# Sketches with the tokens as weights, a split decode and a new order in a sketched-attention and expert-attention kernel

## The chip, the cores and the metric

The kernel runs on one core of a Trainium2 chip. The metric is the device time of one execution in microseconds (us). The engines are PE (TensorE matmuls), PEld (its weight loads, which overlap PE), DVE (VectorE), ACT (ScalarE), POOL (GpSimd) and SP, which here issues most of the DMAs.

## What is computed

Two blocks in a row, for four batches. The first is linear attention on sketches: q and k (4 heads of 32) are projected by S1 and S2 onto 8 numbers each, and their 64 products are the features. The second takes the first one's output as x and computes causal attention for four experts, of which each token takes two.

```python
def phi(x):
    a = np.einsum('rd,bhsd->bhsr', S1, x)
    b = np.einsum('rd,bhsd->bhsr', S2, x)
    return np.einsum('bhsi,bhsj->bhsij', a, b).reshape(*x.shape[:-1], r * r)
q_p, k_p = (phi(q), phi(k))
kv = np.einsum('bhsf,bhsd->bhfd', k_p, v)
z = np.sum(k_p, axis=2)
num = np.einsum('bhsf,bhfd->bhsd', q_p, kv)
den = np.einsum('bhsf,bhf->bhs', q_p, z)[..., None] + 1e-06
x = num / den                       # (4, 4, 1088, 32) -> (4, 1088, 128)
logits = x @ w_gate                 # the two largest of four, softmax over them
for e in range(4):
    scores = scale * (x @ wq[e]) @ (x @ wk[e]).transpose(0, 2, 1)   # causal
    ye = softmax(scores) @ (x @ wv[e]) @ wo[e]
    out += weight_of_e_for_the_token * ye
```

All of it is float32, apart from S1 and S2, which arrive as float64.

## The kernel before

The program is a list of jobs (`job(name, engine, cost, function, reads, makes, holds)`), and `ORDER` is one written-out order of them, which gives every engine its own in-order queue. Words such as `77a` and `17b` are a job's number and which of its possible engines runs it. A buffer of a pool (`in`, `w`, `fp`, `AT`, the four PSUM pairs `ps`) is taken at a holder's first job and given back at its last. Costs and ranks in the jobs are those with which the order was made; at run time only the order counts.

The first batch (b = 0) is prepared alone, before anything else can run, and has its own code (`early`). In order:

- S1 and S2 arrive as pairs of 32-bit words; `decode` (DVE, L302 to L322) makes a high and a low float32 part and transposes them to `SK`, and `spread` copies them to all four row groups.
- k is loaded in two halves by rows (L422), q in twelve pieces (L459), v in four (L435). DVE turns k and q in blocks of 32 x 32 (L499, L511), so that the 32 numbers of a head lie on partitions.
- `sketch` (L538, L550) multiplies with 32 x 32 tiles, S as the weights and the tokens moving, high and low part added in PSUM. DVE turns the results back (L554, L563), and DVE and POOL multiply the features (L560, L568).
- `sums` (L626) adds features times v over tokens, by pairs of heads. It needs k's features and `vp`, which ACT and POOL spread from the loaded v (`spread v`). `keep sums` copies them to `kvz`.
- q's features are transposed on PE (`turn qf`, L669) and copied; `numer` (L689) multiplies them, 128 tokens as weights, by `kvz`; `divide` (L696 to L698), `turn x` (L704) and `keep x` make the turned x of a group of 6 or 5 times 64 tokens.
- The gate's logits (L902) need `wg`, which POOL copies from load w4. DVE compares and chooses (L906 to L948). The choices of group 0 are spread as masks by PE (`widen`); those of groups 1 and 2 go through DRAM (`store masks` L1008, `fetch masks` L1024).

After that the main stream runs per batch and group of tokens: `query` (L1089), `pick` on DVE by the masks (L1102), `score` (L1127), `take` on DVE (L1139, bias and maximum), `exp` on ACT, `weigh` on POOL, `turn A` on DVE (L1175), `sum` on PE (L1203), `out` (L1325). Batch b + 1 is prepared within it by other code (`add low`, `gram`, `fifth`, `numer` at L843). Forty `dummy` jobs (L255) are matmuls on zeros that the order may place on PE, or leave out (`b`).

## Time and profile before

| | us |
|---|---|
| median of 3 runs | 263.31 (262.7 to 264.98) |
| the profiled execution | 263.23 |
| its span | 261.1 |

| engine | busy us | share of the span |
|---|---|---|
| PE | 252.5 | 97% |
| DVE | 206.5 | 79% |
| POOL | 157.6 | 60% |
| ACT | 106.4 | 41% |

The busy times are those of the profiled execution; dummies count as busy. Times in timelines and in the chain count from the start of the span. "Idle before" is the time for which an engine did nothing ahead of an instruction, with what ended it.

### The profile page before, as it was taken

Reading aid. Unit: us, or ns where it says so; the run is one execution under the profiler, and the core shown is the slowest. Engines: PE = TensorE matmul, PEld = TensorE weight load, DVE = VectorE, ACT = ScalarE, POOL = GpSimd, SP = SyncE. Lnnn points to the kernel's source line nnn. Section 1 sums busy time; section 2 is a strip of 40 time slices with the busy share of each in tenths; the row PEclk is TensorE's granted clock in tenths of the full one; section 3 lists DMA queues with packets and bytes.
Section 4 is the critical chain, followed back from the end, with each engine's and each line's share of the span. In section 5 each row is a group of like instructions: output and inputs, shape, how many; then the busy total and the mean of one; then the engine's idle time right before and its main releaser. Section 6 shows DMA issues by size and latency. Waiting matters only on the chain.

```text
span 261.1 us, 9695 instructions
## 1 busy us (share of the span) xinstructions
PE 252.5 (97%) x4028; PEld 189.3 (72%) x4031; DVE 206.5 (79%) x529; ACT 106.4 (41%) x280; POOL 157.6 (60%) x258
## 2 busy tenths in 40 slices
PE   8899899999999999999999989999999999999994
PEld 2686564565598797485689956946796885789994
DVE  4858998999979988989987379999589759972342
ACT  3035653464701704563543145464513614541420
POOL 5850769689676773568963466666475354623470
PEclk9999999999999999999999999999999999999999
DMA  4683839896465329801802599232303059671003
GB/s 143 156 164 89 136 57 252 207 142 114 125 116 108 90 57 203 213 18 53 200 6 36 99 205 189 68 82 66 74 3 86 6 86 227 115 160 25 5 1 85
DMA packets 85467, 27.85 MB, mean 107 GB/s; under 512 B 56624, under 2 KB 84784, under 8 KB 85424
## 3 DMA queue, kind: packets, MB, share of 16 engines
q1 hardware_dynamic: 85120, 26.90, 49.8%
q8 instruction: 31, 0.51, 0.9%
q10 hardware_dynamic: 304, 0.35, 0.5%
q14 instruction: 12, 0.10, 0.1%
HBM read 22.62 MB, written 4.62 MB: 104 GB/s over the span
## 4 chain that ended last, share of the span: by engine, by line
PE 81%; DMA 6%; DVE 4%; SPq 4%; POOL 2%; issue 2%; ACT 0%; ACTq 0%; DVEq 0%; POOLq 0%
PE pair L1203 28%; PE pair L1127 23%; PE pair L1089 9%; PE pair L1325 7%; PE pair L1274 3%; DMA in<-in_q_dram 2%; DMA xd<-w 2%; DMA in<-in_k_dram 1%; PE pair L843 1%; DMA vp<-in_v_dram 1%; PE pair L550 1%; SPq L724 1%; DVE w L1139 1%; PE pair L1300 1%; PE pair L689 1%
## 5 line engine op out<-in xcount | busy, mean ns | idle before, releaser
L1170 POOL TENSOR_SCALAR w<-w,rs,sh 128x128 f32<-128x128 f32 (+15 forms) x68 | 56.1, 830 | 32.8 <-DVE rs L1166 31.4
L1155 ACT ACTIVATE w<-w,mx 128x448 f32<-128x448 f32 (+16 forms) x68 | 52.3, 770 | 56.9 <-DVE mx L1139 40.9
L1127 PE MATMUL pair<-xT,qs 128*128 128x448 f32 (+11 forms) x216 | 73.5, 478 | 0.9 <-DVE qs L1102 0.7
L1127 PEld LDWEIGHTS pair<-xT,qs 128*128 128x128 f32 x216 | 38.1, 190 | 26.1 <-issue 12.4
L1175 DVE STREAM_TRANSPOSE AT<-w 128x256 f32<-128x256 f32 (+14 forms) x68 | 50.8, 759 | 6.4 <-POOL w L1170 6.3
L1139 DVE CUSTOM_DVE_ANT_0 w<-pair,mask 128x768 f32<-128x768 f32 (+13 forms) x68 | 48.0, 723 | 4.5 <-PE pair L1127 3.5
L1203 PE MATMUL pair<-AT,xra 32*128 32x160 f32 (+5 forms) x1136 | 45.0, 302 | 0.0
L1203 PEld LDWEIGHTS pair<-AT,xra 32*128 32x128 f32 x1136 | 42.2, 185 | 3.7 <-DVE mx L1139 0.6
L1230 POOL TENSOR_TENSOR agg<-agg,mb 128x768 f32<-128x768 f32 (+1 forms) x22 | 33.9, 1559 | 13.4 <-ACT agg L197 9.9
L197 ACT COPY agg<-pair 128x384 f32<-128x384 f32 (+1 forms) x38 | 15.9, 469 | 51.6 <-PE pair L1203 41.1
L1089 PE MATMUL pair<-xT,Mq 128*128 128x384 f32 (+1 forms) x96 | 33.5, 474 | 0.1
L1203 PE MATMUL pair<-AT,xrb 32*128 32x160 f32 (+5 forms) x752 | 27.1, 286 | 0.0
L1102 DVE COPY_PREDICATED qs<-mb,pair 128x768 f32<-128x768 uint16 (+1 forms) x24 | 23.1, 961 | 4.6 <-ACT qs L197 2.6
L1203 PEld LDWEIGHTS pair<-AT,xrb 32*128 32x128 f32 x752 | 26.6, 185 | 0.0
L1089 PEld LDWEIGHTS pair<-xT,Mq 128*128 128x128 f32 x96 | 17.5, 190 | 11.1 <-issue 2.4
L568 POOL TENSOR_TENSOR fp<-w 128x576 f32<-128x576 f32 x20 | 23.8, 1204 | 1.9 <-DVE w L563 0.8
L1325 PEld LDWEIGHTS pair<-Mo,agg 128*128 128x128 f32 x168 | 20.1, 192 | 2.0 <-issue 1.0
L1325 PE MATMUL pair<-Mo,agg 128*128 128x128 f32 x168 | 20.7, 276 | 0.0
L1163 POOL TENSOR_SCALAR rs<-zs 128x1 f32<-128x1 f32 x33 | 8.1, 244 | 19.3 <-ACT w L1155 17.2
L1166 DVE RECIPROCAL rs<-rs 128x1 f32<-128x1 f32 x68 | 8.9, 141 | 9.0 <-ACT rs L1161 7.7
L1226 DVE COPY_PREDICATED agg<-mb,pair 128x384 f32<-128x384 uint16 (+1 forms) x24 | 12.5, 554 | 4.3 <-ACT agg L197 4.1
L197 ACT COPY qs<-pair 128x384 f32<-128x384 f32 (+1 forms) x22 | 9.3, 454 | 9.9 <-PE pair L1089 6.5
(180 smaller groups left out, 299.2 us busy)
## 6 DMA issues: line engine op xcount, KB each, us to landing
xra<-xd SPq DMA_DIRECT2D x16, 192.0 KB, 4.4
xrb<-xd SPq DMA_DIRECT2D x16, 192.0 KB, 4.8
xrc<-xd SPq DMA_DIRECT2D x16, 160.0 KB, 5.4
mb<-me SPq DMA_DIRECT2D x3, 576.0 KB, 5.4
mb<-me SPq DMA_DIRECT2D x6, 288.0 KB, 3.8
in<-in_k_dram SPq DMA_DIRECT2D x12, 136.0 KB, 3.5
in<-in_q_dram SPq DMA_DIRECT2D x3, 544.0 KB, 5.6
xd<-w SPq DMA_DIRECT2D x12, 136.0 KB, 3.6
```

Of the source, the lines that this page charges most:

```text
L197: (nc.scalar.copy if eng == "ACT" else VEC[eng].tensor_copy)(o, i)
L568: VEC[e].tensor_tensor(out=f, in0=a[:, :, None, R : 2 * R].to_broadcast([128, NJ, R, R]), in1=a[:, :, 0:R, None].to_broadcast([128, NJ, R, ...
L1089: nc.tensor.matmul(plan[ps[x]][:, y, 0:w], Mq[:, ((1, 2), (0, 3))[x][y]], plan[xT][:, 64 * t0 : 64 * t1], start=True, stop=True)
L1102: nc.vector.copy_predicated(chosen(), rows(c), rows(plan[ps[x]]))
L1127: nc.tensor.matmul(plan[p][:, y, 0 : c1 - c0], plan[qs][:, 128 * t : 128 * t + 128], plan[xT][:, c0:c1], start=True, stop=True)
L1139: nc.vector.tensor_tensor_reduce(out=o, in0=src, in1=msk, scale=-1.0, scalar=mx[:, b, i, x - 1 : x] if x else 3e38, op0=ALU.add, op1=ALU.m ...
L1155: nc.scalar.activation(out=a, in_=a, func=ACTF.Exp, bias=mx[:, b, i, last : last + 1], scale=-1.0, accum_out=zs[:, b, i : i + 1])
L1170: nc.gpsimd.tensor_scalar(out=a, in0=a, scalar1=rs[:, b, i : i + 1], scalar2=plan[("sh", b)][:, i : i + 1], op0=ALU.mult, op1=ALU.mult)
L1175: nc.vector.transpose(dst[:, 0 : keys // 32, t], plan[A][:, 0:keys].rearrange("p (j s) -> p j s", s=32))
L1203: nc.tensor.matmul(plan[Vk[g // 2]][:, g % 2, lo : 32 * nt], plan[(f"xr{j // 12}", b)][rows, j % 12], a[rows, j, lo:], start=(j == 0), sto ...
L1230: nc.gpsimd.tensor_tensor(out=a, in0=a, in1=plan[mb][:, 2 * x : 2 * x + 2, 0:w], op=ALU.mult)
L1325: nc.tensor.matmul(plan[p][0:m, 0, 128 * x : 128 * x + 128], plan[agg][:, e, 128 * x : 128 * x + m], Mo[:, e], start=(e == 0), stop=(e == ...
```

## The change

For the first batch alone:

- The sketches are turned round: 32 turned tokens are the weights (all four heads on 128 rows), and a block-diagonal copy `SB` of S (4 heads x 16 columns, once for the high and once for the low part) moves. The results come out with the tokens on partitions, so the transposes back are gone; `keep ab` copies them, and DVE's features read one operand from PSUM. k is done in two parts (blocks 0 to 4 and 5 to 8), q in three.
- The decode is in two jobs, high part first; `SB` is zeroed and filled by eight small copies. q's first sketch is in two jobs, high part first.
- k is loaded in four parts of 160, 160, 128 and 96 columns twice per row, into a buffer of `AT`, and turned in two parts that match the sketches. Its padding is zeroed before the turn.
- The sums go by token blocks (first five, then four) and no longer by pairs of heads.
- Each numerator's weights are 64 columns twice in place of 128 once.
- `ORDER` is new throughout. In the first 45 us: six dummy jobs lead (eleven matmuls) and none follows until two behind the last output (before: ten lead, ten lie between). v's loads have fifteen SP issues ahead (before fourteen). All of turn qf but one piece stands before the sums; numer 0.0 and 0.1 follow each other; `add low 1.1` is POOL's; load w4 stands behind the four loads of k1; POOL's one-hot and mask stand behind its part of the spread of v; `turn choice 0.1` stands before turn q1.0; the first fetch of x stands right behind the masks' fetches. Behind 57 us PE's groups follow each other as before, with scores and outputs changing places among themselves.

The core of the diff (the order itself and the job declarations are left out):

```diff
-            eng.dma_start(out=dst[:, c0:c1], in_=src[b].rearrange("h (t c) d -> (h t) (c d)", c=C)[:, c0:c1])
+            n, m = x // 2, x % 2
+            w = D * (5 - n - n * m)
+            src = k[b].rearrange("h (t c) d -> (h t) (c d)", c=C).rearrange("p (a y) -> p a y", a=2)
+            dst = plan[kin][:, 0 : 128 * NJ].rearrange("p (a g y) -> p a g y", a=2, g=2)[:, :, m]
+            eng.dma_start(out=dst[:, :, 160 * n : 160 * n + w], in_=src[:, :, 288 * m + 160 * n : 288 * m + 160 * n + w])
...
-                            nc.tensor.matmul(plan[ts[h // 2]][32 * g : 32 * g + 32, h % 2, 0:96], SK[rows, s],
-                                             src[rows, 384 * n + 96 * g : 384 * n + 96 * g + 96], start=(s == 0), stop=(s == 1))
...
+        def sketch_rows(nm, at, step, j0, j1, t, ss):
+            for s in ss:
+                for j in range(j0, j1):
+                    for g in range(4):
+                        c = at + 32 * (step * g + j)
+                        nc.tensor.matmul(plan[t][32 * g : 32 * g + 32, 0, 64 * (j - j0) : 64 * (j - j0) + 64], plan[turned_of(b, nm)][:, c : c + 32],
+                                         SB[:, s].rearrange("p h y -> p (h y)"), start=(s == 0 and j == j0), stop=(s == 1 and j == j1 - 1))
+
+        def keep_ab(e, nm, j0, j1, t):
+            copy(e, plan[ab[nm]][:, 64 * j0 : 64 * j1], plan[t][:, 0, 0 : 64 * (j1 - j0)])
+
+        def multiply(e, nm, j0, j1, at, t):
+            a = plan[ab[nm]][:, 64 * j0 : 64 * j1].rearrange("p (n y) -> p n y", y=16)
+            c = a if e == "POOL" else plan[t][:, 0, 64 * (j0 - at) : 64 * (j1 - at)].rearrange("p (n y) -> p n y", y=16)
...
-        def sums(m):
+        def sums(j0, j1):
...
-                nc.tensor.matmul(plan[t][:, z // 6, c : c + 2 * (D + 1)], f[:, y],
-                                 plan[kvz][:, y % 2].rearrange("p x d -> p (x d)"), start=True, stop=True)
+                for g in range(2):
+                    nc.tensor.matmul(plan[t][64 * g : 64 * g + 64, z // 6, c : c + 2 * (D + 1)], f[:, y, 64 * g : 64 * g + 64],
+                                     plan[kvz][:, y % 2].rearrange("p x d -> p (x d)"), start=True, stop=True)
```

## Rows read from the trace of the kernel before

**Rows 1.** The page, busy time, share and instructions of PE

```profile
PE 252.5 (97%) x4028; PEld 189.3 (72%) x4031; DVE 206.5 (79%) x529; ACT 106.4 (41%) x280; POOL 157.6 (60%) x258
```

**Rows 2.** The chain that ended last: start us, us, what

```profile
14.49 2.46 PE pair L626 x71
...
57.69 2.41 PE pair L1127 x6
```

**Rows 3.** Busy time by stretches: PE, PEld, DVE, ACT, POOL, PEclk, DMA share, GB/s

```profile
17.00:25.00 8.00, 8.00 (x99) 6.23 (x99) 5.69 (x21) 4.51 (x10) 1.10 (x3) 1.00 0.50 123
25.00:33.00 8.00, 7.09 (x81) 4.73 (x72) 7.75 (x26) 4.65 (x9) 5.11 (x12) 1.00 0.77 127
33.00:43.00 10.00, 9.94 (x183) 6.47 (x184) 8.90 (x40) 5.58 (x23) 7.72 (x15) 1.00 0.51 116
43.00:57.50 14.50, 13.86 (x216) 8.69 (x215) 13.51 (x25) 6.17 (x16) 11.99 (x22) 1.00 1.00 206
57.50:257.80 200.30, 198.99 (x3109) 153.99 (x3106) 159.35 (x387) 81.92 (x215) 119.96 (x176) 1.00 0.46 95
```

**Rows 4.** The same for the dummies (L255) alone: PE, then PEld

```profile
25.00:60.00 35.00, 2.35 (x7) 0.78 (x8) 1.00 0.78 153
```

**Rows 5.** Timeline of the start: start us, us, engine, instruction, [idle before]

```profile
4.25 0.23 DVE L322 STREAM_TRANSPOSE SK<-w 32x64 f32<-32x64 f32 x1
...
5.06 0.15 PEld L255 LDWEIGHTS <-idle 128*128 128x128 bf16 x1 [0.28 <-issue]
5.49 0.54 PEld L255 LDWEIGHTS <-idle 128*128 128x128 bf16 x3 [0.28 <-issue]
```

**Rows 6.** Timeline of v and the sums, and the landing of v's loads

```profile
7.54 1.86 SPq L435 DMA_DIRECT2D w<-in_v_dram  x4
DMA to landing us min/median/max: 2.7/3.4/4.1
...
13.17 1.07 ACT L197 COPY vp<-w 128x1024 f32<-128x1024 f32 x1 [8.15 <-DMA w<-in_v_dram]
...
14.49 2.35 PEld L626 LDWEIGHTS pair<-vp,fp 128*64 128x64 f32 x72 [0.42 <-ACT vp L197]
```

**Rows 7.** Timeline of PE: sketches of q, logits, Gram matmuls

```profile
12.44 0.88 PE L538 MATMUL pair<-w,SK 32*32 32x96 f32 x55 [0.71 <-issue]
...
22.70 0.53 PE L902 MATMUL pair<-xT,wg 128*32 128x192 f32 x8
...
31.87 0.35 PE L770 MATMUL pair<-w,bp 128*32 128x32 f32 x18 [0.48 <-DVE qs L1102]
```

**Rows 8.** DMA issues by tile: count, KB each, median us to landing

```profile
in<-in_k_dram SPq DMA_DIRECT2D x1, 272.0 KB, 3.9
...
wgr<-in_moe_w_gate_dram SPq DMA_DIRECT2D x1, 2.0 KB, 4.0
```

**Rows 9.** Timeline of PE's weight loads: one numerator of three

```profile
17.70 1.42 PEld L689 LDWEIGHTS pair<-kvz,fp 128*128 128x128 f32 x12
```

**Rows 10.** Timeline of DVE from the first division to the first pick by fetched masks

```profile
19.30 0.17 DVE L696 TENSOR_SCALAR den<-pair 128x12 f32<-128x12 f32 x1 [0.86 <-PE pair L689]
...
20.24 0.41 DVE L560 TENSOR_TENSOR fp<-w 128x256 f32<-128x256 f32 x1
...
23.38 0.38 DVE L906 STREAM_TRANSPOSE ch<-pair 128x192 f32<-128x192 f32 x1 [0.53 <-PE pair L902]
...
29.75 1.05 DVE L598 TENSOR_TENSOR w<-w 128x288 f32<-128x288 f32 x1
...
33.56 0.30 DVE L997 STREAM_TRANSPOSE cT<-c 64x128 bf16<-64x128 bf16 x1
33.80 0.24 DVE L1139 CUSTOM_DVE_ANT_0 w<-pair,mask 128x128 f32<-128x128 f32 x1
...
43.44 1.01 DVE L1102 COPY_PREDICATED qs<-mb,pair 128x768 f32<-128x768 uint16 x1 [1.04 <-DMA mb<-md]
```

**Rows 11.** Timeline of SP: the masks' two fetches

```profile
36.67 2.29 SPq L1024 DMA_DIRECT2D mb<-md  x2
```

More of the change, by code (lines that the diff above doesn't have):

```diff
@@ L527, in parts_ab, with sketch @@
             return plan[ab[nm]].rearrange("p (h j y) -> p h j y", h=H, j=NJ)
[L529 removed]
+        def sketch(nm, first_, ts):
             src = plan[turned_of(b, nm)]
[L532 to L540 removed]
+            both = nm == "k"
             for s in range(1 if both else 2):
@@ new lines, in sketches, with rows @@
+                    ("ah", nm, b, x) if nm == "k" else ("ab", nm, b, x), [ts[x], ab[nm]], rank=at + 0.5 + 0.1 * x)
+        def rows(nm, x, at, step, j0, j1, cuts_, need, r):
+            t, n = ("ps", "sk", nm, x), 64 * (j1 - j0)
+            base = j0 if nm == "k" else 0
+            cut = ((0,), (1,)) if nm == "q" and x == 0 else ((0, 1),)
+            for ss in cut:
+                last = ss[-1] == 1
+                job(f"sketch {nm}{b}.{x}" + ("" if last else " hi"), "PE", 0.13 * (j1 - j0) * len(ss), lambda e, ss=ss: sketch_rows(nm, at, step, base, base + j1 - j0, t, ss),
+                    [*need, *[("SB", s) for s in ss], *([("skh", nm, b, x)] if ss == (1,) else [])],
+                    ("sk" if last else "skh", nm, b, x), [turned_of(b, nm), t], mode="L", rank=r)
+            job(f"keep ab {nm}{b}.{x}", ("ACT", "DVE"), (a_us(n), d_us(n)), lambda e: keep_ab(e, nm, j0, j1, t),
+                [("sk", nm, b, x)], ("ab", nm, b, x), [t, ab[nm]], rank=r + 0.05)
+            for y, (c0, c1) in enumerate(cuts_):
+                w = 256 * (c1 - c0)
+                job(f"features {nm}{b}.{x}.{y}", ("DVE", "POOL"), (0.12 + w / 960, 0.12 + 0.00184 * w), lambda e, c0=c0, c1=c1: multiply(e, nm, c0, c1, j0, t),
+                    [("ab", nm, b, x)], ("fp", nm, b, x, y), [t, ab[nm], fps[nm]], rank=r + 0.2 + 0.1 * y)
@@ L618, in prepare @@
-        kvb = ("ps", "kv", b)
-        def sums(m):
-            t = plan[kvb][:, 0, 0 : 2 * (D + 1)].rearrange("p (m d) -> p m d", m=2)
-            kp = plan[fps["k"]].rearrange("p (j h f) -> p j h f", h=H, f=R * R)
-            for j in range(NJ):
-                for x in range(2):
-                    h = 2 * m + x
-                    nc.tensor.matmul(t[64 * x : 64 * x + 64, m], kp[:, j, h], plan[vp][:, j, h, :],
+        if early:
+            for x in range(2):
+                rows("k", x, 0, 9, kcuts[x][0][0], kcuts[x][1][1], kcuts[x], [("kT", b, x)], rank(0.05 + 0.01 * x))
+            for n in range(3):
+                rows("q", n, 384 * n, 3, 3 * n, 3 * n + 3, ((3 * n, 3 * n + 2), (3 * n + 2, 3 * n + 3)),
+                     [("qT", b, n), *([("clear", "q")] if n == 2 else [])], rank(0.17 + 0.1 * n))
+        else:
+            at = rank(0.05)
+            sketches("k", at, lambda: SKk, ["SKk", *lead_fp])
+            for x in range(2):
+                job(f"add low {b}.{x}", ("POOL", "DVE"), (0.65, 0.4), lambda e, x=x: add_low(e, x), [("ah", "k", b, x)],
+                    ("ab", "k", b, x), [ab["k"]], rank=at + 0.6 + 0.1 * x)
+            for h in range(H):
+                engs = ("POOL", "DVE")
+                job(f"features k{b}.{h}", engs, tuple(fus[e] for e in engs), lambda e, h=h: features(e, "k", h),
+                    [("ab", "k", b, h // 2)], ("fp", "k", b, h // 2), [ab["k"], fps["k"]], rank=at + 1 + 0.1 * h)
```

241 lines of the change are left out of this document (107 added, 134 removed).

## The prediction

> **What bounds the kernel now.** I read the busy shares first, then the chain that ended last, then busy time by stretches, and last the timelines of the first 45 us. PE is busy for 97% of the span [rows 1]: all that can be won is time in which PE does nothing, does dummies, or does work that the change shortens. From 57.69 us on the chain is PE to the end [rows 2], and in the 200.3 us from 57.5 to 257.8 PE is idle for 1.3 us [rows 3]. So the end comes when PE gets into its steady stream, plus 200 us that the diff hardly touches (its new order keeps the sequence of groups there). The question is how much earlier PE passes 57.7 us.
>
> Between 17 and 25 us PE has no gap. In the three stretches from 25 to 57.5 it is idle for 0.91, 0.06 and 0.64 us [rows 3], and eight dummies lie there (eight weight loads in [rows 4]), at 0.21 us each (three start within 0.43 us in [rows 5]) another 1.7 us. So PE has 3.3 us of slack there, while DVE is busy for 7.75 of 8, 8.90 of 10 and 13.51 of 14.5 us [rows 3]: DVE's list is what PE waits for.
>
> What sets the start of that list? The chain enters PE with the sums at L626, 14.49 us [rows 2]. They wait for ACT's spread of v, and ACT waited 8.15 us for v's DMA: four issues from 7.54 to 9.40 us, each 2.7 to 4.1 us to landing, the spread at 13.17, the sums at 14.49 [rows 6].
>
> **The change part by part.**
>
> *Start.* The dummies end near 6.5 us now; the new order has eleven matmuls of them ahead of the first sketch. At the slower pitch of 0.43 us up to 5.49 and at 0.21 after it [rows 5] they end at about 5.7. The decode's high part has nine of twelve small operations, so its transpose comes some 0.35 us earlier than the present one at 4.25 [rows 5]; block copies and turn q0.0 follow, and the first sketch starts near 5.7, where the first one now starts at 7.0.
>
> *Sketches.* Removed: 64 matmuls of k and 192 of q, and eight DVE transposes of the results. Added: two instructions per float32 matmul, 2 parts x 9 blocks x 4 rows of tokens x 2 = 144 for k and 144 for q, each with 32 columns of weights over 128 rows, and 64 columns moving. No row has this form. Bounds: 16 ns (55 of q's present matmuls in 0.88 us) and 66 ns (8 of the logits', with such weights but 192 columns moving, in 0.53 us); 18 Gram matmuls, with such weights and 32 columns, take 0.35 us, 19 ns each [rows 7]. I take 20 ns, as 64 columns are nearer to the Gram's 32: 5.8 us in all. k's second load, seventh on SP, issues at about 3.4 us and lands at most 3.9 later, the time of the present half [rows 8]; with 60% of its bytes I take 2.9. Its turn ends near 7.2, and the 240 instructions behind it end at 12.0, not at 13.3 as now [rows 7].
>
> The Trainium skill (TensorE: Matmul & The Clock Gate, section "Wait — 56ns, not 53.3ns?") says that matmuls never start closer together than about 25 ns, however small: by that the 288 would take 7.2 us, an estimate from that page. The trace has 16 ns for tiles of 32 columns, so the rule does not hold for them.
>
> *But the sums need v.* SP now has fourteen issues before v's four, and then fifteen; at 0.46 us an issue v comes 0.4 us later. So the sums start at about 14.9 whatever the sketches gain: their 1.3 us is cover and worth nothing by itself (were v there, it would be worth up to that). The sums in two halves by token block are the same 72 instructions, 2.35 us [rows 6].
>
> *At nothing:* blank, eight block copies, the copies of the sketches and the features lie on DVE, ACT and POOL before the spread of v, which hides them with some 2 us to spare; without that cover the longest, POOL's four features, are about 4.4 us.
>
> *Numerators.* Three times 12 instructions with 128 columns of weights and 66 moving take 1.42 us, 118 ns each [rows 9]. After: 24 with 64 columns. The sums' weights have 64 columns too: 33 ns each [rows 6], which gives 0.79; the other bound is no gain, 1.42. I take 0.85, since the row with equal weights is the nearer one: 0.55 saved, three times, 1.7 us of PE.
>
> *From the sums to the first take (L1139, now 33.80).* The sums end near 17.3 (now 16.9); turn qf 0.2.0 covers their copies; numerator 0.0 ends at about 18.9, and its division starts at 18.95 instead of 19.30, 0.35 earlier. From there DVE's new list has three divisions, the turns of k1 and q1, the choices and two picks. Two pieces that stand there now are gone: features q0.1.1 (0.41, ahead of the sums) and add low (1.05, on POOL) [rows 10], with their overlap about 1.3 us. Of the wait of 0.53 us for the logits some 0.2 stays: 0.3. Together the first take comes 1.95 us earlier, at 31.85. POOL has idled long before that point, so add low there delays nobody that I see.
>
> *Masks.* The turn of the second choice (L997) stands before turn q1.0 and comes at about 31.1, not 33.56 [rows 10]. SP then needs as now some 2.8 us until it fetches the masks at 36.67 [rows 11]; so the pick at 43.44, which waited 1.04 us for them [rows 10], can go at about 41.0. DVE's own list, 8.6 us from first take to 42.4, ends at 40.5. Gain at the pick: 2.4, and with the rest of that wait shared by the next picks 2.7. Moved on SP: x's first fetch stands right behind the masks' and waits for a store to land, with stores and q2 behind it; by the same issue times the four fetches are out by 43.5 us, some 4 before now.
>
> *PE* must follow. It has 3.3 us of slack, the numerators' 1.7, and three transposes' groups (about 0.9) that it now does while it waits for v, less 0.4 for the later sums: up to 5.5 us. So DVE's 2.7 are kept at 57.7 us, and the rest is PE as before.
>
> Sum: 0.35 + 1.3 + 0.3 + 0.75 (masks and picks) = 2.7 us off the profiled execution's 263.23 (its span of 261.1 and 2.1 around it): 260.5. The median of the runs, 263.31, is 0.1 from that execution.
>
> **The rivals.**
>
> *A, the lead is eaten on the way.* The gate's weights (load w4) now stand behind four loads of k1: issue near 16.5 us, 4.0 to landing [rows 8], then POOL's copy: 20.8, for logits at 21.9. It decides when it comes over 1.1 us later. For it: POOL's mask and one-hot, moved behind the wait for v, stand in the same queue. Against: the room of 1.1 us. The gain falls to about 0.8: 262.4.
>
> *B, the clock.* Without dummies PE pauses from about 13.5 to 14.9, longer than any pause now. The pitch shows both levels: 1.2 GHz until 5.49 us, some 4.2 us after PE began, then 2.4 [rows 5]. If the pause brings the lower one back, about 4.2 us run at half speed, 2.1 lost: 262.6. Against: a pause of 0.71 us [rows 7] did not do it. [...]
>
> *C, slower: the sketches become the bound.* The sums need 240 instructions behind 5.7 us, with 0.6 us of other work between. Over 36 ns each they end after v. At 66 ns they end at 22.1, the sums at 24.5 instead of 16.9, 7.6 later, of which the numerator's 0.55 and DVE's 2.35 come off: 267.9. Slower than before from 46 ns, by 1% from 57. For it: the logits' row. Against: the Gram's and q's [rows 7].
>
> *D, PE uses all its slack*, as DVE gets ahead too (in this reckoning it waits for some 6 us before 19): 5.3 us, 257.9.
>
> **How the numbers follow.** Forecast (gain of 1.5 to 4): 0.56. A: 0.17. B: 0.08. C: 0.08. D: 0.11. 1% of 263.3 is 2.6 us, about what a measurement of this kernel can tell from no change, and the forecast lies on that line: 0.37 of its 0.56 above it, with D 0.48 faster. Same: the other 0.19, A, and most of B, 0.43. Slower: C and a little of B, 0.09. The range reaches from D to the first prices of C: 257.9 to 263.6.
>
> **What would show it.** Right: the sums start at 14.5 to 15.2 behind ACT's spread of v; 24 instructions of a numerator in 0.8 to 0.9 us; the first take near 32; the first pick behind the masks near 41. Wrong: sums that wait for features or sketches (C), a doubled pitch after 14 us (B), DVE idle before the logits' turn (A), a new wait of PE after 60 us, which no row of before prices.

## The result, and the profile after

| kernel | median us (runs) | ratio to before, 95% interval |
|---|---|---|
| before, beside it | 263.0 (262.5 to 264.98, 6) | 1 |
| after | 266.63 (265.58 to 267.73, 6) | 1.0130 (1.0085 to 1.0175) |

The change made the kernel 1.3% slower; the forecast was 260.5, with a range of 257.9 to 263.6. The profiled execution of after took 267.01 us, its span is 264.9 (before: 263.23 and 261.1). Executions that took over 1.5% longer than the fastest of their kernel are left out of the medians and ratios below, and in sfirst, both and oldfill128 the profiled execution is such a one, so of these only the first 45 us are read.

The page of after; the lines are busy time by engine, and the granted clock of PE in 40 slices:

```profile
PE 252.5 (95%) x4084; PEld 189.6 (72%) x4085; DVE 209.4 (79%) x539; ACT 106.4 (40%) x281; POOL 156.3 (59%) x254
PEclk9599999999999999999999999999999999999999
```

PE is busy for 252.5 us in both kernels [rows 1]: the 3.8 us of longer span are idle time. And one slice, the second, has half the clock.

Busy time by stretches of after (PE, PEld, DVE, ACT, POOL, PEclk, DMA share, GB/s); the last two answer to lines of [rows 3]:

```profile
7.00:12.00 5.00, 4.35 (x126) 4.15 (x130) 3.71 (x8) 0.04 (x1) 2.41 (x6) 0.57 0.70 167
12.00:14.50 2.50, 2.50 (x105) 2.50 (x100) 0.44 (x2) 0.74 (x2) 1.50 (x2) 0.50 0.65 128
...
33.00:43.00 10.00, 8.63 (x193) 5.52 (x193) 9.57 (x34) 5.08 (x21) 7.37 (x12) 1.00 0.43 90
...
57.50:257.80 200.30, 197.30 (x3144) 151.03 (x3112) 162.27 (x396) 81.29 (x213) 121.39 (x173) 1.00 0.48 94
```

From 33 to 43 us PE is idle for 1.37 us instead of 0.06, and behind 57.5 for 3.0 instead of 1.3 [rows 3]: the second was to stay as it was.

Timeline of PE at the start of after (start us, us, engine, instruction, [idle before <- what ended it]):

```profile
7.65 1.50 PE L566 MATMUL pair<-SB,w 128*32 128x64 f32 x48 [2.37 <-DVE w L531]
9.08 1.06 PE L365 MATMUL pair<-ident,rep 32*128 32x32 f32 x4
10.07 5.66 PE L566 MATMUL pair<-SB,w 128*32 128x64 f32 x240
15.66 1.75 PE L687 MATMUL pair<-ident,fp 128*128 128x128 f32 x14
17.34 2.63 PE L645 MATMUL pair<-vp,fp 128*64 128x33 f32 x72
```

The first sketch starts at 7.65, not 5.7. PE had stood for 2.37 us, and from 8 to 14 us its granted clock was 0.50 (1.2 GHz): 240 sketches take 5.66 us, 23.6 ns each. There is no gap between the sketches, the transposes of q's features and the sums: the sums (17.34; 14.49 in [rows 2]) come when PE's queue reaches them.

The other engines in the same stretch of after: SP's load of S and of v, DVE's first step of the decode, its transpose of the high part and its turn of the first q, ACT's spread of v, then DVE's first take and first pick by fetched masks:

```profile
1.44 0.52 SPq L241 DMA_DIRECT2D w<-in_S_dram  x1
8.98 1.84 SPq L453 DMA_DIRECT2D w<-in_v_dram  x4
...
4.10 0.17 DVE L311 TENSOR_SCALAR w<-w 32x32 int32<-32x32 int32 x1 [2.41 <-DMA w<-in_S_dram]
...
5.41 0.20 DVE L320 STREAM_TRANSPOSE SK<-w 32x32 f32<-32x32 f32 x1
...
6.92 0.58 DVE L531 STREAM_TRANSPOSE w<-in 128x384 f32<-128x384 f32 x1
...
16.02 1.07 ACT L198 COPY vp<-w 128x1024 f32<-128x1024 f32 x1
...
35.88 0.29 DVE L1158 CUSTOM_DVE_ANT_0 w<-pair,mask 128x128 f32<-128x128 f32 x1
...
44.79 1.01 DVE L1121 COPY_PREDICATED qs<-mb,pair 128x768 f32<-128x768 uint16 x1 [0.26 <-DMA mb<-md]
```

S is there 1.15 us later than before, whose timeline of DVE has

```profile
2.95 0.17 DVE L310 TENSOR_SCALAR w<-w 32x32 int32<-32x32 int32 x1 [1.76 <-DMA w<-in_S_dram]
```

V is issued 1.44 later (8.98; 7.54 in [rows 6]), the first take is 2.1 later and the pick 1.35 later ([rows 10]: 33.80 and 43.44). The numerators are as forecast: 48 instructions in 1.63 us and 24 in 0.92.

One table of starts, read from the timelines of one execution each, says where the kernels below stand (us; "stream" is the first instruction of `sum` in four of its nine blocks, the last of which starts some 30 us before the end):

| | first sketch | sums | first take | pick by masks | stream 1 | stream 5 | stream 6 | last |
|---|---|---|---|---|---|---|---|---|
| before | 7.01 | 14.49 | 33.80 | 43.44 | 52.5 | 134.4 | 166.0 | 231.1 |
| after | 7.65 | 17.34 | 35.88 | 44.79 | 54.0 | 137.3 | 169.5 | 234.7 |
| fill | 8.81 | 17.09 | 35.36 | 44.93 | 54.0 | 138.9 | 169.7 | 234.9 |
| fill7 | 7.90 | 16.63 | 35.43 | 44.24 | 53.5 | 137.0 | 168.2 | 233.4 |
| nolow | 7.73 | 15.63 | 33.84 | 43.46 | 52.4 | 136.3 | 167.1 | 232.3 |
| oldstream | 7.55 | 15.75 | 33.96 | 43.26 | 52.9 | 135.4 | 167.8 | 232.9 |
| oldfill | 7.47 | 15.28 | 33.82 | 43.25 | 53.1 | 135.6 | 167.4 | 232.5 |
| newstream | 7.30 | 15.02 | 34.16 | 43.38 | 52.5 | 135.9 | 166.7 | 231.9 |
| numer64 | 7.10 | 14.47 | 33.04 | 43.36 | 52.5 | 134.8 | 167.1 | 232.2 |
| masks64 | 7.66 | 14.80 | 33.47 | 41.99 | 51.2 | 133.7 | 167.8 | 232.9 |
| masks128 | 6.35 | 14.33 | 33.81 | 42.32 | 51.5 | 133.4 | 164.7 | 229.8 |

After is 1.5 us late at 54.0, 2.9 at 137, 3.5 at 169, and no later from there on. So three places have to be explained: the lead, the stream up to 137, and something between 153 and 169.

One execution is a coarse measure of the lead. After and oldstream run the same program up to the first numerators, and their sums stand at 17.34 and 15.75; fill7, oldfill, unlock and unlockm share another lead, and theirs stand at 16.63, 15.28, 18.58 and 16.82. A difference of a us or two at the sums is therefore not by itself the work of an edit.

### The profile page after: what moved, and what is told of

Read it like the earlier page. It is cut to its first block, busy times and chain, and to the rows that moved or that the text cites. A ratio compares the mean times of both kernels' runs of the same rounds, so it can differ in the third digit from the quotient of the medians.

```text
span 264.9 us, 9826 instructions
## 1 busy us (share of the span) xinstructions
PE 252.5 (95%) x4084; PEld 189.6 (72%) x4085; DVE 209.4 (79%) x539; ACT 106.4 (40%) x281; POOL 156.3 (59%) x254
## 4 chain that ended last, share of the span: by engine, by line
PE 73%; DVE 10%; DMA 7%; issue 3%; POOL 3%; ACT 1%; SPq 1%; DVEq 0%; POOLq 0%
PE pair L1222 23%; PE pair L1146 22%; PE pair L1344 7%; PE pair L1108 6%; PE pair L1293 3%; DMA mb<-md 3%; DMA mb<-me 3%; PE pair L566 3%; DVE w L1158 2%; DVE qs L1121 1%; ACT agg L198 1%; DVE w L580 1%; PE pair L1319 1%; DVE fp L840 1%; DMA w<-in_S_dram 1%
## 5 line engine op out<-in xcount | busy, mean ns | idle before, releaser
L1146 PE MATMUL pair<-xT,qs 128*128 128x384 f32 (+10 forms) x216 | 74.6, 479 | 2.7 <-DVE qs L1121 1.4
L1174 ACT ACTIVATE w<-w,mx 128x128 f32<-128x128 f32 (+15 forms) x68 | 52.4, 771 | 54.6 <-DVE mx L1158 51.7
L1189 POOL TENSOR_SCALAR w<-w,rs,sh 128x192 f32<-128x192 f32 (+15 forms) x68 | 56.6, 839 | 27.3 <-DVE rs L1185 23.9
L1194 DVE STREAM_TRANSPOSE AT<-w 128x192 f32<-128x192 f32 (+15 forms) x68 | 50.9, 759 | 5.6 <-POOL w L1189 5.3
L1158 DVE CUSTOM_DVE_ANT_0 w<-pair,mask 128x256 f32<-128x256 f32 (+13 forms) x68 | 48.6, 725 | 6.8 <-PE pair L1146 5.5
L198 ACT COPY agg<-pair 128x384 f32<-128x384 f32 (+1 forms) x36 | 14.6, 469 | 53.2 <-PE pair L1222 46.2
L1108 PE MATMUL pair<-xT,Mq 128*128 128x384 f32 (+1 forms) x96 | 34.6, 477 | 1.2 <-DVE rs L1185 0.7
L585 POOL TENSOR_TENSOR fp<-w 128x576 f32<-128x576 f32 x21 | 24.4, 1177 | 0.4
L1182 POOL TENSOR_SCALAR rs<-zs 128x1 f32<-128x1 f32 x34 | 7.2, 211 | 27.1 <-ACT w L1174 19.0
L1174 ACT ACTIVATION_READ_ACCUMULATOR w<-w,mx 128x1 f32 x68 | 12.8, 188 | 0.0
```

What stands on the lines that cost most here:

```text
L198: (nc.scalar.copy if eng == "ACT" else VEC[eng].tensor_copy)(o, i)
L585: VEC[e].tensor_tensor(out=f, in0=a[:, :, None, R : 2 * R].to_broadcast([128, NJ, R, R]), in1=a[:, :, 0:R, None].to_broadcast([128, NJ, R, ...
L1108: nc.tensor.matmul(plan[ps[x]][:, y, 0:w], Mq[:, ((1, 2), (0, 3))[x][y]], plan[xT][:, 64 * t0 : 64 * t1], start=True, stop=True)
L1146: nc.tensor.matmul(plan[p][:, y, 0 : c1 - c0], plan[qs][:, 128 * t : 128 * t + 128], plan[xT][:, c0:c1], start=True, stop=True)
L1158: nc.vector.tensor_tensor_reduce(out=o, in0=src, in1=msk, scale=-1.0, scalar=mx[:, b, i, x - 1 : x] if x else 3e38, op0=ALU.add, op1=ALU.m ...
L1174: nc.scalar.activation(out=a, in_=a, func=ACTF.Exp, bias=mx[:, b, i, last : last + 1], scale=-1.0, accum_out=zs[:, b, i : i + 1])
```

## The experiments

| run | median us (runs) | ratio to before, 95% interval |
|---|---|---|
| fill | 267.86 (4) | 1.0192 (1.0124 to 1.0260) |
| sfirst | 266.08 (6) | 1.0113 (1.0073 to 1.0154) |
| both | 265.53 (2) | 1.0114 (1.0027 to 1.0200) |
| oldstream | 265.17 (6) | 1.0087 (1.0053 to 1.0120) |
| fill7 | 265.68 (6) | 1.0110 (1.0072 to 1.0149) |
| newstream | 263.96 (12) | 1.0032 (1.0013 to 1.0050) |
| numer64 | 264.63 (8) | 1.0053 (1.0025 to 1.0082) |
| lead2 | 268.22 (6) | 1.0192 (1.0167 to 1.0218) |
| nolow | 264.67 (4) | 1.0106 (1.0061 to 1.0150) |
| oldfill | 264.45 (11) | 1.0065 (1.0034 to 1.0097) |
| masks64 | 265.07 (9) | 1.0077 (1.0048 to 1.0106) |
| oldfill128 | 266.23 (6) | 1.0123 (1.0081 to 1.0165) |
| masks128 | 262.22 (12) | 0.9982 (0.9954 to 1.0009) |
| unlock | 264.11 (11) | 1.0030 (1.0005 to 1.0055) |
| unlockm | 264.49 (10) | 1.0064 (1.0030 to 1.0097) |

The medians of before beside them lie between 262.5 and 263.1. Where intervals overlap, the totals don't separate two kernels, and what is said rests on the timelines.

### Is it the clock? fill, sfirst, both

Three edits of after: more dummies ahead of the first sketch (fill), S loaded ahead of k (sfirst), and S first with five more dummies (both).

```diff
-        m = 2 if x < 20 else 1
+        m = 12 if x == 36 else 2 if x < 20 else 1       # fill; both: 6
-SP: load k0.0, load S0, load q0.0.0 ...
+SP: load S0, load k0.0, load q0.0.0 ...                 # sfirst, both
```

> The changed kernel with eleven more dummy matmuls in the sixth dummy job, so that PE has work until the first sketch (7.65 us), nothing else. Clock theory (the pause of 2.37 us before the first sketch brings the clock down to half from 7.7 to 14.3 us, the sketches end 3.7 us late and all of the loss of 3.6 us hangs on it): granted clock 1.00 throughout, the sums start near 15.4 instead of 17.34, and the time falls by 2 to 3.5 us, to 263.2 to 264.6. Order theory (the lead costs 1.4 us at 57.7 us, and the new order loses another 2.2 us in the stream behind it): the lead gains up to 2, but the idle time of PE behind 57 us stays near 3.5 us, and the time is above 264.5. Form theory (128-row weights of 32 columns cost 23 ns an instruction at either clock): the sums stay at 17.3, the time at 266.6.

> The changed kernel with SP's load of S1 issued ahead of the first load of k, nothing else. S landed at 4.10 us in the changed kernel and at 2.95 before. Clock theory: the decode starts 1.1 us earlier, the first sketch near 6.5, the pause of PE shrinks to 1.2 us; if that is short enough the clock stays and the time falls by 2.5 to 4 us (262.6 to 264.1); if it still falls, by about 1.1 (265.5). Order theory: 265 or more. Form theory: 1.1 us earlier at the sums, 265.5.

> S1 loaded first and the pause that is left filled with five dummy matmuls. Clock theory: granted clock 1.00 throughout, first sketch near 6.5, sums near 14.9 (then v sets them), time 262.5 to 263.5. Order theory: sums near 14.9 as well, but 264.5 or more, from PE's idle time behind 57 us. Form theory: sums near 16.2, 265.5.

Fill kept the clock at 1.00 in every stretch and gained nothing: its dummies ended too late (first sketch 8.81), and yet its sketches, at 16 ns each, ended only 0.25 us sooner than in after (15.48 and 15.73). PE stood in the middle of them (timeline of PE in fill):

```profile
8.81 0.88 PE L566 MATMUL pair<-SB,w 128*32 128x64 f32 x48
9.62 0.63 PE L365 MATMUL pair<-ident,rep 32*128 32x32 f32 x4
10.17 2.32 PE L566 MATMUL pair<-SB,w 128*32 128x64 f32 x148
13.95 1.53 PE L566 MATMUL pair<-SB,w 128*32 128x64 f32 x92 [1.46 <-issue]
```

Sfirst brought the first sketch to 6.35, 1.3 us earlier, so the late S is 1.3 of the 1.95 us by which 7.65 missed the forecast (lead2, which loads S first too, has 6.11). The rest lies on DVE. In after the high part takes 1.31 us from its first operation to its transpose (4.10 to 5.41), no less than the whole decode of before (2.95 to 4.25, [rows 5]), and the low part and three copies of `SB` stand ahead of the turn of q at 6.92. But the sums came at 17.04: four v issues took SP 2.93 us and v was the last (timelines of SP and ACT in sfirst):

```profile
9.13 2.93 SPq L453 DMA_DIRECT2D w<-in_v_dram  x4
...
15.87 1.06 ACT L198 COPY vp<-w 128x1024 f32<-128x1024 f32 x1 [2.43 <-DMA w<-in_v_dram]
```

In both, v was spread at 14.97 and the sums came at 16.13; its total, of two executions, is not told apart from that of after. So with a whole clock, with an early start and with both of them the sums still come 1.6 us or more behind those of before (14.49): something stands behind each of them.

### What stands behind: fill7, nolow

Fill7 is after with the rightly sized fill (m = 8, which ends when the first turned q is there). Nolow is fill7 without the low part of S in k's sketches and in those of q's second and third group, so its output is that of a rougher S and PE has 120 sketches (1.9 us) less to do.

```diff
-            for s in ss:
+            for s in ss[:1]:                             # nolow
```

> The changed kernel with seven more dummy matmuls ahead of its first sketch (eight for two... eight in place of one at that place), sized from the run fill, where eleven more at 0.32 us apart ended at 8.8 and the clock stayed whole: seven end at about 7.6, when DVE has turned the first k. Clock theory (half clock from 7.7 to 14.3 is the lead's loss): sketches at 16 ns instead of 23.6, last sketch about 13.8 instead of 15.7, v's sums 15.8 to 16.2 instead of 17.34, first take about 34.5, and 265.4 against 266.6. Landing theory (v lands at 14.9 whatever the sketches do, and what is behind 57 us is the order's): no more than 1 us earlier at the sums, 265.6 to 266.6. Theory that the clock is nothing here: 266.6.

> The changed kernel with the fill of the run fill7 (eight dummy matmuls in place of one ahead of the first sketch), and with the low part of S left out of the first batch's sketches (of k's, and of q's second and third group), so that the first batch's sketch matmuls fall from 288 records to 168; its output is that of a rougher S. In the runs fill, fill7 and lead2 TensorE stood 1.2 to 2.0 us on 'issue' after the same 222 matmuls of the program. Supply theory (TensorE has run out of fetched instructions there, and the twice as many sketches of the change are what brings it to that point inside the sketches): no such stall before the last sketch, sketches end at 12 to 13 instead of 15.0, the sums at 14.5 to 15.5 instead of 16.63 (then v's landing sets them), and the stall, if any is left, stands behind the sums; 264 to 265. Arrival theory (q's last turn on VectorE and v set the end whatever TensorE has to issue): last sketch and sums within 0.4 us of fill7's, 265.7.

Timeline of PE in fill7, then of PE and ACT in nolow:

```profile
9.26 2.33 PE L566 MATMUL pair<-SB,w 128*32 128x64 f32 x152
13.59 1.44 PE L566 MATMUL pair<-SB,w 128*32 128x64 f32 x88 [2.00 <-issue]
14.95 1.75 PE L687 MATMUL pair<-ident,fp 128*128 128x128 f32 x14
16.63 0.94 PE L645 MATMUL pair<-vp,fp 128*64 128x33 f32 x25
```

```profile
10.17 1.58 PE L566 MATMUL pair<-SB,w 128*32 128x64 f32 x80 [0.31 <-DVE w L531]
12.30 1.72 PE L687 MATMUL pair<-ident,fp 128*128 128x128 f32 x14 [0.54 <-DVE fp L577]
15.63 2.29 PE L645 MATMUL pair<-vp,fp 128*64 128x33 f32 x72 [1.61 <-POOL fp L577]
...
14.47 1.06 ACT L198 COPY vp<-w 128x1024 f32<-128x1024 f32 x1 [2.33 <-DMA w<-in_v_dram]
```

In fill7 the sums come 0.7 us earlier than in after, and the median is 0.9 lower; neither is more than the executions and the intervals leave open. Its sketches would have ended at 13; they stood 2.00 us on "issue". In fill, fill7 and lead2 the stall comes behind the same count of matmul records: 22, 18 and 11 dummies, 4 of `rep`, and 196, 200 and 207 sketches, 222 each time. The kernel before has it at the same count, 0.71 us in [rows 7]: 17 dummies, 4 of `rep`, 64 sketches of k and 137 of q. It is in fourteen of the seventeen traces, behind 222 or 223 records, and lasts 0.29 to 2.30 us; it is missing in after and oldstream, where the clock is low there, and in nolow. In each of the fourteen one transfer of the instruction queue (on the page of after 32 packets, 0.52 MB, 16 KB each) starts 2.2 to 3.0 us ahead of the stall's end, among the loads of k and v: at 9.84 in before, 11.16 in fill, 10.72 in fill7, 9.44 in lead2. After shows no such stall: there the transfer starts at 11.27, and at 1.2 GHz PE gets to that point when the instructions are there. So the fall of the clock and the stall cover each other, and curing one uncovers the other.

Nolow, with fewer records in front of the sums (204), has no stall ahead of them; its sketches end at 11.8, and ACT waits for v until 14.47, 1.3 us later than in [rows 6]; the sums stand at 15.63. Its ratio (1.0106) is not told apart from fill7's (1.0110), and oldfill below, with all its sketches, has its sums earlier. That the stall is a wait for instructions is argued from the count, the transfer and nolow; no run changed the transfer itself.

The sketches are not twice as many, as the expectation for nolow has it, but 288 records where before has 64 and 192. What the change does is to put more work behind the stall: from its end to the sums PE has 55 sketches and 6 transposes in before, 2.05 us with a wait for v at the end, and 88 sketches and 14 transposes in fill7 and oldfill, 3.04 and 3.06 us.

### The order of the stream: oldstream, newstream, oldfill

Oldstream is after up to the first numerators, and then the order of before. Newstream is before up to there, and then the order of after. Oldfill is oldstream with fill7's dummies.

```diff
 ORDER: words 1 to 360 of after
-       the rest of after                # oldstream: the rest of before, without its dummies
 ORDER: words 1 to 360 of before
-       the rest of before               # newstream: the rest of after
```

> The changed kernel whose order is the new one up to the second batch's numerator (57 us) and from there the order of before, dummies left out. The clock still falls at 7.7 us. Order theory: PE's idle time behind 57 us falls from about 3.5 to 1.3 us, and the time to 264 to 264.8, 1.4 above before. Clock theory: the lateness comes from the lead, and the order behind 57 us does nothing: 266 to 267.

> The kernel before, in its own order up to the first numerators (about 57 us), and from there on in the changed kernel's order; nothing else is changed. Order theory (the order behind 57 us costs what the run oldstream gave back, 266.6 less 265.2): 264.4 to 265, with more TensorE idle time behind 57 us (1.3 there in the kernel before, about 3 expected). Lateness theory (the stream only passes on that it starts late, and amplifies it): 263, the same as before.

> The run oldstream (the changed kernel up to the first numerators, the order of before behind them) with the fill of the run fill7, so that the clock stays at 2.4 GHz in the lead. If clock (0.95 by fill7) and order (1.4 by oldstream) add up: 264.2 to 264.5, 1.1 to 1.4 over the kernel before, which is then the lead's own (instruction stall and later v). If the lead is swallowed at the masks' pick (43.26 in oldstream with the clock low, 43.44 in the kernel before): 265.2, no different from oldstream.

The new order alone costs 0.8 us in a kernel that is on time until 52.5 (newstream, 0.3%, interval above 1), and taking it out of fill7 lowers the median by 1.2 (oldfill), where the intervals overlap. The prediction had said that it "keeps the sequence of groups there". PE's waits, timeline of PE in newstream and then in after:

```profile
70.25 1.88 PE L1127 MATMUL pair<-xT,qs 128*128 128x480 f32 x4 [0.72 <-DVE mx L1139]
...
116.96 2.39 PE L1274 MATMUL pair<-agg,Mo 128*128 128x320 f32 x8 [0.64 <-POOL w L1170]
```

```profile
71.61 1.88 PE L1146 MATMUL pair<-xT,qs 128*128 128x480 f32 x4 [0.73 <-DVE mx L1158]
...
118.41 2.39 PE L1293 MATMUL pair<-agg,Mo 128*128 128x320 f32 x8 [0.70 <-POOL w L1189]
```

Two waits that before does not have, at the same two places in both kernels. They are not lateness handed on: newstream is on time when it meets them. Between stream 5 and 6 the new order gives 0.8 back in newstream, where the pick waits 0.26 us for the second masks; after, where it waits 1.62, does not get it.

### The numerators: numer64, oldfill128

Numer64 is before with nothing but the numerators by 64 columns of weights; oldfill128 is oldfill with those by 128.

```diff
-  nc.tensor.matmul(plan[t][:, z // 6, c : c + 2 * (D + 1)], f[:, y], kv, ...)
+  for g in range(2):
+    nc.tensor.matmul(plan[t][64 * g : 64 * g + 64, z // 6, c : c + 2 * (D + 1)], f[:, y, 64 * g : 64 * g + 64], kv, ...)
```

> The kernel before with the first batch's numerators by 64 columns of weights and nothing else changed: two matmuls of 64 columns in place of one of 128, in the old order. My step in the prediction: the twelve groups of numerators fall from 1.42 to 0.85 us each, which the page's chain feels at most in the 2 to 3 us where numerators stand between takes; 262 to 263. Theory that weights of 64 columns cost elsewhere (twice the instructions, more instruction fetch): 263 to 264.5.

> The run oldfill (the changed kernel's lead with the clock held, the order of before behind the first numerators) with the first batch's numerators by 128 columns of weights again. oldfill is left 1.5 over the kernel before (264.47 against 262.91), with its first masks' pick at 43.25, no later than before. If the numerators by 64 columns cost what they cost alone in numer64 (0.5% of the fast runs), or what masks64 shows, by moving the work ahead of the masks' landings: 263 to 263.5. If the 1.5 is the sketches' and the loads' (the lead): 264.5 to 265.5, for the numerators then come 0.6 later each.

In numer64 the numerators did what was forecast (0.92 instead of 1.42 for a third of them), and the first take came 0.76 us earlier. Then it was gone, and the kernel ends 0.5% slower than before, with its interval above 1 (timelines of DVE, PE and SP in numer64):

```profile
33.04 0.24 DVE L1140 CUSTOM_DVE_ANT_0 w<-pair,mask 128x128 f32<-128x128 f32 x1
43.36 1.01 DVE L1103 COPY_PREDICATED qs<-mb,pair 128x768 f32<-128x768 uint16 x1 [1.72 <-DMA mb<-md]
...
44.42 0.59 PE L255 MATMUL pair<-idle 128*128 128x512 bf16 x2 [1.21 <-DVE rs L1167]
...
33.96 3.32 SPq L725 DMA_DIRECT2D xd<-w  x4
37.39 0.96 SPq L1025 DMA_DIRECT2D mb<-md  x2
```

The choices were stored 0.77 us earlier than in before, but the masks were fetched at 37.39, 0.72 later than in [rows 11]: four stores of x stand between on SP, and one of their issues took 1.9 us. (In before it is the fetch's own issue that is slow: 1.70 us, to 38.37; in numer64 the first fetch is out at 37.77 and its masks are picked no earlier for it. The masks' flight counts beside the queue.) The pick by masks stands at 43.25 to 43.44 in before, numer64, newstream, oldstream and oldfill, with the take at 33.04 to 34.16. Behind it numer64 loses 0.4 us up to stream 5 and 0.7 up to stream 6, where its pick waits 1.48 us for the second masks. In the changed kernel the numerators look better: the median of oldfill128 is 1.8 us over that of oldfill, but the intervals overlap.

### The masks: masks64, masks128

Numer64 and before, each with the first masks' two fetches ahead of two of those stores.

```diff
 SP: store masks 0, store x 0.2.3, store x 0.0.1,
+    fetch masks 0.1, fetch masks 0.2,
     store x 0.1.0, store x 0.0.3,
-    fetch masks 0.1, fetch masks 0.2,
```

> The run numer64 (the kernel before with its numerators by 64 columns of weights) with the two fetches of the first masks moved on SP's queue ahead of two of the four stores of x that stood before them. In numer64 the logits came 0.76 us earlier and the pick by masks not at all (43.36 against 43.44), and TensorE stood 1.2 us for it. Theory that SP's queue holds the masks: the fetch is issued at about 35.4 instead of 37.39, lands at 41.2 to 41.5, the pick stands at 41.5 to 42, and 261.5 to 262.5. Theory that the masks' own flight (6 us, 1 MB among other transfers) sets it: the pick at 42.5 or later and 263 to 264.

> The kernel before with only the two fetches of the first masks moved ahead of two of the four stores of x on SP's queue, numerators by 128 columns. In masks64 that move brought the first masks' pick from 43.36 to 41.99 and the work at 51 us 1.3 us ahead of the kernel before, and the end 1.9 later: the second batch's masks landed at 154.0 as ever, TensorE stood 1.6 us, and its clock was 0.50 from 157 to 160. If it is the lead itself that is paid back there: pick at 42.5, work at 51 us 0.5 to 1 ahead, a wait for the second masks of 1 us or more, 262.5 to 264. If it is the numerators by 64 columns that cost: 262 to 262.7.

The queue was what held them: fetched at 35.51 and 35.84, picked at 41.99 and 42.32, and the stream begins 1.3 and 1.0 us ahead of before. In masks128 this lead lasts (229.8 at the last block, 1.3 ahead; median 262.22 beside 262.53, which the interval doesn't separate from no change). In masks64 it does not. The two kernels differ in nothing but the numerators, and their intervals do not overlap: 64 columns cost here, not gain. Timelines of DVE and PE in masks64 from 154 us, and one stretch of it (columns as above):

```profile
154.04 2.13 DVE L1103 COPY_PREDICATED qs<-mb,pair 128x768 f32<-128x768 uint16 x2 [1.62 <-DMA mb<-me]
...
156.32 3.31 PE L1128 MATMUL pair<-xT,qs 128*128 128x448 f32 x6 [1.61 <-DVE qs L1103]
```

```profile
157.00:158.00 1.00, 1.00 (x3) 0.51 (x2) 1.00 (x5) 0.00 (x0) 0.66 (x2) 0.50 1.28 162
```

and the same place in before and in masks128:

```profile
153.87 2.17 DVE L1102 COPY_PREDICATED qs<-mb,pair 128x768 f32<-128x768 uint16 x2 [0.70 <-ACT w L1155]
156.18 2.07 PE L1127 MATMUL pair<-xT,qs 128*128 128x448 f32 x6 [0.73 <-DVE qs L1102]
```

```profile
152.53 2.17 DVE L1102 COPY_PREDICATED qs<-mb,pair 128x768 f32<-128x768 uint16 x2 [0.40 <-DMA mb<-me]
```

This is the third place: the next batch's masks (`mb<-me`). From issue to pick they took 6.2 us in masks128, 6.5 at most in before (where the pick waited for ACT), 7.3 in numer64, 7.4 in masks64, 7.8 in after (150.16 to 157.98, a wait of 1.62). The DMA share there is over 1. Where they come late, PE stands, and in masks64 its clock fell on top, so six scores took 3.31 instead of 2.07 us. What makes these 576 KB take 6.2 us in one kernel and 7.4 in another, and what the numerators have to do with it, is open.

### The lead once more: lead2, unlock, unlockm

Lead2 is oldstream with S first, two loads on ACT's queue, v issued ahead of q's last group, v spread ahead of a copy of sketches on ACT, and one of PE's transposes (turn qf 0.2.1) behind the sums.

```diff
 SP:  load S0, load q0.0.*, load k0.1, load q0.1.*, load k0.2, load k0.3,
+     load v0.0 ... load v0.3,
      load q0.2.*,
-     load v0.0 ... load v0.3,
 ACT: load S1, +load k0.0, +load q0.0.1 ...; +spread v0 ahead of keep ab q0.2
 PE:  sums 0.0, sums 0.1, +turn qf 0.2.1 behind them
```

> The changed kernel with the order of before behind 57 us (as in oldstream) and a mended lead: S is loaded ahead of k, two loads go by ScalarE's queue, v's four are issued before the last group of q, v is spread ahead of ScalarE's copy of the last query sketch, and the last query sketch's turn stands behind v's sums on TensorE. If the lateness of the sums (17.34 in the changed kernel, 14.49 before) is that of v's landing and of what is queued ahead of the spread and the sums: sums at 14.5 to 15, first take 32.5 to 33.5, and 262 to 263.5. If the lead is bound by the features and the takes whatever v does: oldstream's 265.2 again.

V was spread at 12.97, in time for sums at 14.1. They came at 17.64 and the kernel was the slowest of all: q's last group was now late, PE stood 1.21 us on issue and 1.28 for its turn, its clock fell to 0.52 between 14.5 and 17, and the sums waited in PE's own queue behind sketches and transposes. The load that is moved back decides what is moved forward.

Unlock and unlockm go after another step. In every run with the lead of after, one DVE operation of the second choice (128 x 22, L964 in after) took 1.04 or 1.05 us, which takes 0.17 in before; there are ten such runs, oldfill among them. Timelines of DVE and POOL in after, and of POOL and DVE in before:

```profile
33.00 1.05 DVE L964 TENSOR_TENSOR c<-c 128x22 bf16<-128x22 bf16 x1
...
32.84 1.18 POOL L585 TENSOR_TENSOR fp<-w 128x576 f32<-128x576 f32 x1
```

```profile
29.31 1.18 POOL L568 TENSOR_TENSOR fp<-w 128x576 f32<-128x576 f32 x1
...
33.36 0.17 DVE L945 TENSOR_TENSOR c<-c 128x22 bf16<-128x22 bf16 x1
```

In after it ends when POOL's product ends (34.02). In before it is `add low` (29.75 to 30.80 in [rows 10]) that lies under POOL's product (to 30.49). In masks64, where `add low` starts further ahead of that product's end (29.20, the product to 30.16), it takes 1.27 us, and again it ends 0.31 behind the product. Unlock is oldfill with the choice ahead of a pick on DVE; unlockm has the earlier masks too.

```diff
 DVE: choose a0.1,
+     choose b0.1,
      pick 0.0.0,
-     choose b0.1,
      pick 0.0.1, turn choice 0.1
```

> The run oldfill with one exchange on VectorE's queue: the second choice's five bfloat16 operations (L960 to L964) stand ahead of the first pick of group 0 and no longer behind it. In all runs with the changed kernel's lead the last of these, 128 x 22 numbers with both inputs in SBUF, took 1.04 us where the kernel before has 0.17, and it ended each time as GpSimd's product of k1's features (1.18 us, begun 0.16 us before it) ended. Blocking theory (a VectorE operation with two inputs in SBUF stands while GpSimd reads there): in its new place, some 0.8 us before that product begins, it takes 0.17 to 0.2, the first take comes 0.85 earlier (33.0 instead of 33.82), and 263.6 to 264.5, as far as the masks let it through. Theory that the operation is slow of itself here (its operands or its place behind the choice): 1.04 again and 264.5.

> The run unlock with the two fetches of the first masks moved ahead of two stores of x on SP's queue, as in masks64 and masks128. If the lead gained on VectorE is held up only by the masks (pick at 43.25 in oldfill with the take at 33.82): first take 33.0, pick by masks 41.3 to 42.3, and 262 to 263.5, no slower than the kernel before. If the second batch's masks near 155 us take it back, as in masks64: 264 to 265 with a wait of 1.5 us or more there.

In both, L964 took 0.17 and 0.18 us, and first division to first take took 13.8 us instead of 14.3: 0.5 of the 0.85 expected. Most of the rest is lost where the two picks now follow each other: they start 1.13 us apart, where in oldfill the operation behind the first pick starts 0.91 behind it. The first take of unlock itself stood at 36.26, not at 33.0: in that execution the stall on issue took 2.30 us, the clock fell behind it, and the sums came at 18.58. Unlock's median is 1.0 over that of before and oldfill's 1.5, but their intervals overlap. Unlockm did not come down to 262 to 263.5 (264.49): the masks' pick stood at 43.91, since in that execution the stall on issue (1.90 us) had the sums at 16.82, and the second masks were waited for by 1.28 us again.

## Why the prediction was wrong, point by point

*What bounds the kernel.* Right for the stretch to 57.7, and the lateness there (1.4 us) is carried to the end. "The rest is PE as before" failed: 2.1 us more were lost behind it in the trace of after: 1.4 up to stream 5, as in newstream (1.5), and 0.6 between stream 5 and 6, where newstream wins 0.8 back and after waits for the second masks. The order was read as a sequence of groups, not as queues; whether PE meets a finished `take` or `weigh` at 71 and 118 us was no part of it.

*Start: first sketch at 5.7.* Measured 7.65. The step left S where it was, but SP's load of S now stands behind one of k that takes 0.66 us to issue (1.44 instead of 1.17), and S landed 1.15 later. Sfirst shows the price, 1.3 us at the first sketch. The nine operations of the high part ran to 5.4, not to 3.9: besides the late S they took as long as all twelve of before, and the low part's four operations, which stand ahead of the turn of q, are not named in it.

*Sketches: 20 ns, last end 12.0.* The size was right for the whole clock, even pessimistic: 16 ns (152 in 2.33). The length of the stretch was wrong twice over: at 1.2 GHz 23.6 ns, and at 2.4 GHz a stall of 0.5 to 2.3 us in the middle. Before has that stall too, behind the same count of records, 0.71 us [rows 7]; the forecast put it at nothing without a reason. C, sketches as the bound, was argued from the rate alone; at 16 ns the stall, the sketches behind it and the transposes became the bound.

The Trainium skill (TensorE: Matmul & The Clock Gate, section "Wait — 56ns, not 53.3ns?") has a floor near 25 ns between matmuls; 16 ns with weights of 128 x 32 and 64 columns moving is below it, as the forecast's row for small tiles was.

*v: 0.4 us later.* Measured 1.3 (nolow, where nothing else is waited for: 14.47 against 13.17). The step took 0.46 us an issue; k's four took 0.55 to 0.66 each, v's issue came 1.44 later and v's landing up to 4.3. And "the sums start at about 14.9 whatever the sketches gain" turned out the other way round: the sketches and the transposes behind them were last. So the transposes that were moved ahead of the sums ("that it now does while it waits for v") filled no wait; they made the sums later.

*Numerators 0.85.* Right: 0.8 to 0.9. That they would save time as a whole failed where they are tried alone: numer64 is 0.5% slower than before.

*First division to first take: 1.6 us less.* Measured 0.2 less (14.31 against 14.50). So of the 4.0 us by which the first take missed the forecast (35.88, not 31.85), 2.6 were there at the first division (21.57, not 18.95) and 1.4 arose here. The 1.05 us of add low were taken for its work. They were mostly a wait under POOL's product (a product of 128 x 256 takes 0.41 in [rows 10]), and the new list puts another operation with two inputs in SBUF under the same product (1.05; unlock: 0.17 out of its way). The Trainium skill (SBUF — State Buffer, section "Who interferes with whom") says that a DVE instruction with two SBUF inputs contends with a GpSimd instruction that reads SBUF; these traces agree, 1.04 against 0.17 us. The row stood in [rows 10]; POOL's row of the same time (29.31, 1.18 us), which says what it is, was left out of the reckoning.

*Masks: pick at 41.0.* The mechanism, SP's 2.8 us from choice to fetch, was taken as a fixed time. It is the time of the stores between, and those stretch: a choice 0.77 earlier gave a fetch 0.72 later (numer64). With the fetch ahead of two stores 1.45 of the 2.4 us at the pick were there (41.99 in masks64), of which 1.1 need no earlier choice (masks128).

*The rivals.* B was the right mechanism at a place not thought of: the fall came behind the 2.37 us in which PE waits for the first turned q, not behind the sketches. Its price is not shown: by medians 0.9 us lie between after and fill7, whose intervals overlap. A did not happen: the logits' turn (25.77) waited 0.37 for ACT's copy of x, not for the gate's weights. D, more gain from slack, was far off: slack on PE is not what was short.

In sum, by medians after is 3.6 over before. Two parts of the change have a run of their own in a kernel that is otherwise before, and each makes it slower with an interval above 1: the order (newstream, 0.3%) and the numerators by 64 columns (numer64, 0.5%). The lead is left. S late, the fall of the clock, the stall on issue with more work behind it, v late and the operation under POOL's product are each seen in the traces, but fill7, nolow, oldfill and unlock are not told apart by their totals, so the share of each in the 3.6 us is not shown.

## What to carry to other kernels

Price an edit in a queue by what the queue meets next: here a stall behind a count of instructions, an engine that reads beside it and another issue on SP each took part of a gain, and curing one late thing showed the next. Run the same program more than once before a difference of a us at its start is put down to an edit. A duration in a trace is not the work of the operation until the engines beside it have been looked at. In a kernel whose later stages wait for transfers of their own (here the masks at 43 and 155 us), follow a gain to those transfers before it is counted, and check that the transfer's issue moves with it.

## What the runs showed of the hardware

PE's clock did not follow the length of a pause alone. It fell to 0.50 behind 2.37 us (after), 1.68 us (oldstream), 1.61 us (masks64, at 155) and 2.30 us on issue (unlock), and not behind 1.46, 1.90 and 2.00 us on issue (fill, unlockm, fill7). Timeline of PE and a stretch of unlock (columns as above):

```profile
14.07 0.80 PE L566 MATMUL pair<-SB,w 128*32 128x64 f32 x21 [2.30 <-issue]
...
14.50:17.00 2.50, 2.50 (x84) 2.33 (x75) 0.69 (x1) 0.67 (x3) 0.03 (x1) 0.50 0.83 161
```

Nolow has both: 1.61 us ahead of the sums without a fall, and a fall behind 31 to 33 us, where PE was busy for 0.65 of 2 us. After has the same 0.65 of 2 us from 33 to 35, and no fall behind it. Two stretches of nolow, then two of after:

```profile
31.00:33.00 2.00, 0.65 (x36) 0.44 (x35) 2.00 (x3) 1.05 (x3) 2.00 (x2) 1.00 0.20 35
33.00:35.00 2.00, 2.00 (x8) 1.41 (x8) 1.65 (x9) 0.80 (x4) 0.10 (x1) 0.66 0.12 18
...
33.00:35.00 2.00, 0.65 (x35) 0.45 (x34) 2.00 (x3) 1.05 (x3) 2.00 (x2) 1.00 0.06 12
35.00:37.00 2.00, 1.98 (x40) 1.50 (x41) 1.97 (x11) 0.75 (x4) 0.14 (x1) 1.00 0.05 5
```

The Trainium skill (TensorE: Matmul & The Clock Gate, section "HAM oscillation — how this bites in real kernels") blames pauses; these are shorter than those it tells of. In after, behind the 2.37 us, PE worked some 6.6 us at 1.2 GHz (7.7 to 14.3) before 2.4 came back.

- Float32 matmuls with weights of 128 x 32 and 64 columns moving follow each other at 16 ns at 2.4 GHz.
- A DVE operation with both inputs in SBUF stood for 0.9 us under a POOL product, in ten kernels alike.
- In before too PE stands on issue behind 222 matmul records, and where a program is run again the stall takes another length: 1.04 (oldfill), 1.90 (unlockm), 2.00 (fill7) and 2.30 us (unlock) with one and the same start.
- One issue on SP can take 1.7 to 1.9 us instead of 0.4 (the first fetch of masks at 36.67 in before, a store in numer64): no row says what it waits for.
